# Sinkhorn attention and routed experts on one core: the first w1 load, the order of mixes, batch-0 logits, x sums and PSUM pools rearranged

## The chip, the cores and the metric

The kernel runs on one core of a Trainium2 chip. The metric is device time of one execution in microseconds (us), the median of several runs. A core has five engines that issue independently: TensorE (PE) with its weight loads (PEld), VectorE (DVE), ScalarE (ACT), GpSimd (POOL) and SyncE (SP). The last two also issue the DMAs here, each on a queue of its own. Every engine works through its instructions in the order in which they are queued.

## The reference

Two stages. Attention over 4 batches, 8 heads, 768 positions of 64: a matrix P per head (8 x 8 blocks of 96 positions) is normalised five times by rows and columns, the blocks of k and v are mixed by it, and each block of q attends to its mixed block. Then a mixture of 8 experts over the 3072 resulting rows x of 512, every expert on every row:

```python
k_sorted = np.einsum('bhij,bhjcd->bhicd', P, k_b)
v_sorted = np.einsum('bhij,bhjcd->bhicd', P, v_b)
attn = softmax(scale * q_b @ k_sb.T)          # per block of 96
x = (attn @ v_sb) as [3072, 512]
P = np.exp(x @ w_gate - max)                  # [3072, 8]
for _ in range(8):                            # rows, then columns
    P /= P.sum(1) + 1e-9; P /= P.sum(0) + 1e-9; P *= N / E
for e in range(E):
    out += P[:, e:e+1] * (np.maximum(x @ w1[e], 0) @ w2[e])
```

(Shortened: the softmax stands for the reference's max, exp and division.)

## The kernel before

**Head (0 to 36 us).** Batch 0 of the attention is done at once in two halves b of four blocks each, with pairs of heads hp, on PSUM tiles of two banks each (pool `ps0`, four tiles used in turn, handed out by `pair()`). Its steps are written out by hand in a string (L486): `s` is `half_scores` (matmuls, then the exponential on ACT), `m` is `half_mix` (attention times v, then reciprocal and product on DVE), `t` is `half_turn` (transposes into `xtT`, which holds x transposed), `h` is `half_hidden` (the first layer of expert 0, 256 of its 1024 columns at a time), `v` is `sort_pair` for batch 1 (the mixing of v by P), `k` `wide_keys`, `p` the spreading of P for all batches with the loads of batch 1 and of w2. In `s03` the digits are b and hp; in `h01` b and the group of columns. `unread` names the steps that are preceded by one matmul on a blank tile whose result nobody reads (`warm`).

**The hop.** `sort_values` and `sort_pair` leave the mixed v in `vs` with 16 partitions for each block; `hop` moves it by DMA into `vsbt`, with each block's 96 positions on 96 partitions. For batch 0 it is cut into twelve DMAs, five issued by SP and seven by POOL. POOL's DMA queue has been given before that, in this order: q, v, k of batch 0, `w_gate`, and the first half of w1 of expert 0 (`load_w1(0, 0, 512)`, L99). The rest of w1 and batch 1's v are held behind `gate`, a POOL copy that reads the first two pieces of the hop (L478 to L482).

**Middle (36 to 110 us).** Batches 1 to 3 of the attention, on single banks from a pool of eight (`pa`), are woven with expert 0's layers on the batches before (`first_two`, `weave`, `run_both`). `attention` takes its plan from a string as well (L544, L552): `q` queries, `k` keys, `s` scores, `m` mix, `t` turn, `l` logits; the commas join steps that stand between two steps of the other stream. The logits (x times `w_gate`) of batch 0 are the first work on `pa` (L543).

**Experts 1 to 7.** These use Strassen's form with seven products in place of eight, which needs sums of quarters of x (`sum_x(p)`, p the group of 1024 rows: four DVE instructions, three into `xc`, the fourth in place in `xtT`), of w1 (`sum_w`, POOL), of w2 (`sum_w2`, POOL) and of the hidden layer (`sum_h`, POOL). The first three of `sum_x(0)` are traced in batch 3's part of the loop (L568), the fourth in the first step of the next stage (`works`, L802), which also carries the normalisation of the gate (`balance`, called `chain`) and expert 0 for the last two batches (`last_two`). From there PSUM is split into `bk`, five banks for the first layer, and `op`, three for the second (L583 to L586). The seven experts then follow in one loop, from some 170 us to the end.

**What sets the order.** `pin` is `tc.keep_in_program_order`: the instruction stays behind the one that was traced before it on the same engine. Instructions that are not pinned, `sum_x`'s among them, are put by a scheduler where it takes their engine to be free and their inputs ready, and so may stand far ahead of their place in the text. `reuse_waits="tile"` makes a tile of a new pool wait for those tiles of the old pool that lay on the same memory, and for no others.

Of the kernel before, what the change touches and what calls it, by code (L numbers as in the profile page):

```python
# [17 lines left out]
ALU = mybir.AluOpType  # L18
# [7 lines left out]
def kernel(  # L26
# [11 lines left out]
    nc = tc.nc  # L38
    B, H, S, D = 4, 8, 768, 64
    NB, BL = 8, 96  # L40
    N, Dm, E, F = 3072, 512, 8, 1024
    NT = 24
    TB = S // 128
# [20 lines left out]
    pin = tc.keep_in_program_order  # L64
# [14 lines left out]
    def load_w1(e, f0=0, f1=F):  # L79
        if e not in w1t:  # L80
            w1t[e] = wp.tile([128, 4, F], BF16, name="w1e")
        pin(nc.gpsimd.dma_start(
            out=w1t[e][:, :, f0:f1],
            in_=moe_w1[e].rearrange("(kk k) f -> k kk f", k=128)[:, :, f0:f1]))
# [11 lines left out]
    load_batch(0, [(x, l0, 4) for x in "vk" for l0 in (0, 4)])  # L96
    wg = ones.tile([128, 4, E], BF16)
    pin(nc.gpsimd.dma_start(out=wg, in_=moe_w_gate.rearrange("(kk k) e -> k kk e", k=128)))
    load_w1(0, 0, 512)  # L99
    blank = perp.tile([128, 512], BF16)  # L100
    nc.vector.memset(blank, 0.0)
    mask16 = ones.tile([128, 16], F32)
# [17 lines left out]
    def sum_x(p):  # L120
        if p not in xc:
            xc[p] = xcp.tile([128, 3, 2, 512], BF16, name="xc", bufs=2)
        ta, tb = (slice(1024 * p + 512 * i, 1024 * p + 512 * i + 512) for i in range(2))
        b11, b12, b21, b22 = (xtT[:, k:k + 2, t] for k in (0, 2) for t in (ta, tb))
        x1, x2, x4 = (xc[p][:, j] for j in range(3))
        for a, b, c in ((b12, b11, x1), (b22, x1, x2), (b21, x2, x4), (b22, b12, b12)):
            nc.vector.tensor_tensor(out=c, in0=a, in1=b, op=ALU.subtract)
            yield

    Pb = perp.tile([128, 32, 8], F32)  # L130
# [73 lines left out]
                                  kps.rearrange("p kk (i c) -> p i c kk", i=8))  # L204

    at = {}

    def new_at(bb, hp, h):
        at[bb, hp, h] = sp.tile([128, NB, 96], BF16, name="atp", bufs=8)
# [155 lines left out]
    def attention(bb, bank, plan):  # L365

        def step(what, hp):
            if what == "q":
                queries(bb, hp, bank)
            elif what == "k":  # L370
                keys(bb, hp, bank)
            elif what == "s":
                scores(bb, hp, bank)
            elif what == "t":
                turn(bb, hp, bank, nc.vector.tensor_copy)
            elif what == "l":
                logits(bb, bank, (0, 1, 2) if hp == 0 else (3,))
            else:
                for h in range(2):
                    mix(bb, hp, h, bank)  # L380

        for some in plan.split():
            for x in some.split(","):
                step(x[0], int(x[1]))
            yield
# [41 lines left out]
    with tc.tile_pool(name="ps0", bufs=4, space=bass.MemoryType.PSUM,  # L427
                      reuse_waits="tile") as ps0:
        pair = lambda: ps0.tile([128, 2, 512], F32, name="pair")
        warm(pair(), 11)  # L430
        rs = pp.tile([32, 8], F32)
        cs = pp.tile([32, 8], F32)
        Pt = P.rearrange("p i j -> p j i")
        nc.vector.reduce_max(out=rs, in_=P, axis=AX.X)
        nc.vector.tensor_sub(P, P, mkap(rs, [rs.ap[0], rs.ap[1], [0, 8]]))
        for it in range(5):


            pin(nc.scalar.activation(out=P, in_=P, func=AF.Exp))
            if it == 3:  # L440
                warm(pair(), 3)
            for hp in {2: (0, 1), 3: (2,), 4: (3,)}.get(it, ()):
                wide_queries(hp, pair)
            if it == 1:
                pin(nc.vector.reduce_sum(out=mask16, in_=Ibig.rearrange("p (j c) -> p c j", c=16),
                                         axis=AX.X))
            pin(nc.vector.reduce_sum(out=rs, in_=P, axis=AX.X))
            nc.vector.reciprocal(out=rs, in_=rs)
            nc.vector.tensor_mul(P, P, mkap(rs, [rs.ap[0], rs.ap[1], [0, 8]]))
            nc.vector.reduce_sum(out=cs, in_=Pt, axis=AX.X)  # L450
            if it == 0:
                nc.vector.tensor_scalar_add(cs, cs, 1e-9)
            nc.vector.reciprocal(out=cs, in_=cs)
            nc.vector.tensor_mul(Pt, Pt, mkap(cs, [cs.ap[0], cs.ap[1], [0, 8]]))

        Prep = perp.tile([32, 8, 8, 16], BF16, name="R1")
        for eng, i0, n in ((nc.vector.tensor_copy, 0, 5), (nc.scalar.copy, 5, 3)):
            eng(Prep[:, i0:i0 + n], mkap(P, [P.ap[0], [8, n], [1, 8], [0, 16]], off=i0 * 8))

        def spread(n):  # L460
            t = pair()
            warm(t, n)
            pbps = t[:, 0, 0:256].rearrange("p (i g) -> p i g", i=8)
            for i in range(8):
                pin(nc.tensor.matmul(pbps[:, i, :], Prep[:, i].rearrange("p j c -> p (j c)"),
                                     Ibig[0:32, 0:32], start=True, stop=True))
            return pbps

        build_r(0, nc.vector, 2, spread(12))
        S_, G_ = nc.sync, nc.gpsimd  # L470
        for hp in range(4):
            sort_pair(0, hp, pair)
            if hp == 1:
                hop(0, [(S_, 0, 0, 4), (G_, 1, 0, 4), (S_, 2, 0, 4), (G_, 3, 0, 4)])
        wide_keys(0, pair)
        hop(0, [(S_, 0, 4, 4), (G_, 1, 4, 4), (G_, 2, 4, 4), (G_, 3, 4, 4),
                (S_, 4, 0, 8), (G_, 5, 0, 8), (G_, 6, 0, 8), (G_, 7, 0, 8)])
        gate = nc.gpsimd.tensor_copy(  # L478
            held, mkap(vsbt[0], [[VW, 96], [520, 2]], off=259))
        with tc.issue_after(gate.ins):  # L480
            load_w1(0, 512, F)
            load_batch(1, [("v", 0, 8)])  # L482
        wide_keys(1, pair)
        halves = [mps.tile([128, 8, 384], BF16, name="hTs") for _ in range(2)]
        unread = {"s03": 1, "m00": 1, "m01": 1, "m02": 1, "m03": 1, "m10": 1, "m11": 1}
        for x in ("s00 k2 s01 k3 p s02 s03 s10 m00 s11 m01 s12 m02 s13 m03 t00 m10 m11 t01 m12 "  # L486
                  "h00 m13 h01 t10 h02 t11 h03 v0 v1 v2 v3 h10").split():
            n = [int(c) for c in x[1:]]
            if x[0] == "s":
                half_scores(*n, pair, unread.get(x, 0))  # L490
            elif x[0] == "m":
                half_mix(*n, pair, unread.get(x, 0))
            elif x[0] == "t":
                half_turn(*n, lambda: ps0.tile([128, 2048], BF16, name="pair"),
                          nc.vector.tensor_copy if x == "t11" else nc.scalar.copy)
            elif x[0] == "h":
                half_hidden(*n, halves[n[0]], pair)
            elif x[0] == "v":
                sort_pair(1, *n, pair)
            elif x[0] == "k":  # L500
                wide_keys(*n, pair)
            else:
                nc.vector.tensor_copy(Pb, spread(0).rearrange("p i g -> p g i"))
                build_r(1, nc.gpsimd, 4)
                load_batch(1, [("k", 0, 8), ("q", 0, 4), ("q", 4, 4)])
                load_w2(0)
        hop(1)
# [10 lines left out]
    with ExitStack() as c2:  # L518
        pa = c2.enter_context(tc.tile_pool(name="pa", bufs=8, space=bass.MemoryType.PSUM,
                                           reuse_waits="tile"))  # L520
        bank1 = lambda shape, dt: pa.tile(shape, dt, name="bank", tag="bank")
# [18 lines left out]
                next(a, 0)  # L540
                run(n)

        logits(0, bank1, (0, 1, 2, 3))  # L543
        at1 = attention(1, bank1, "k0 k1 k2 q0 q1 s0 q2 s1 k3 q3 s2 "  # L544
                                  "m0 s3 m1,t0 m2,t1 m3 t2 t3,l0 l3")
        run_both(at1, (1, 1, 1, 1, 0, 1, 0, 1, 0, 0, 2))
# [4 lines left out]
        run_both(at1, (1, 0, 1, 0))  # L551
        usual = "q0,q1,k0 k1,s0,q2 k2,s1,q3 m0 k3,s2 m1,t0 s3 m2,t1 m3 t2 t3,l0 l3"  # L552
        for bb, ns in ((2, (5, 3, 2, 4)), (3, (5, 4, 0, 5))):
            at1 = attention(bb, bank1, usual)
            weave(at1, ex, 5, ns[0])
            if bb + 1 < B:
                load_batch(bb + 1, [(x, 0, 8) for x in "vkq"])
                build_r(bb + 1, nc.gpsimd, 4)
            else:
                load_w1(1)  # L560
                sums = sum_w(1)
            weave(at1, ex, 3, ns[1])
            if bb + 1 < B:
                weave(sort_values(bb + 1, bank1), ex, 5, ns[2])
            else:
                for _ in sums:
                    pass
                x0 = sum_x(0)  # L568
                for _ in range(3):
                    next(x0)  # L570
            weave(at1, ex, 4, ns[3])
        for _ in ex:
            pass
# [6 lines left out]
    osp = late("osp", 1)  # L580
    htp, fsp, hsp, w2q = late("htp", 2), late("fsp", 1), late("hsp", 3), late("w2q", 1)
    h3p = late("h3p", 2)
    bk = ctx.enter_context(tc.tile_pool(name="bk", bufs=5, space=bass.MemoryType.PSUM,  # L583
                                        reuse_waits="tile"))
    op = ctx.enter_context(tc.tile_pool(name="op", bufs=3, space=bass.MemoryType.PSUM,
                                        reuse_waits="tile"))  # L586
    osbl[1] = osp.tile([128, 6, Dm], F32, name="osbl1")
    load_w2(1)
# [294 lines left out]
```

## Time and profile before

| | us |
|---|---|
| median of 3 runs | 675.48 (675.46 to 680.38) |
| the profiled execution, device time | 675.74 |
| its span in the profile | 673.5 |
| PE busy | 660.1 (98%) |
| DVE busy | 544.3 (81%) |
| POOL busy | 473.0 (70%) |
| ACT busy | 296.1 (44%) |

The span runs from the first to the last instruction; device time has 2.2 us more around it. The profile is that of one execution. Its views are: busy time by engine and by stretch; the groups of instructions by source line; the waits, that is, whose idle time was ended by whom; the chain of work that ended last, traced back from the end; the timeline of single instructions; and the DMA issues with the time from issue to landing. `L153` is line 153 of the kernel; `out<-in` names the tiles that an instruction writes and reads. The granted clock of TensorE in this run was 0.999 of full speed over the span.

### The profile page before, as it was taken

To read this page: it belongs to the slowest core of one execution; us is meant where nothing else is said; L and a number is where in the kernel's file an instruction comes from. 1 tells how busy PE (TensorE), PEld (TensorE's weight loads), DVE (VectorE), ACT (ScalarE), POOL (GpSimd) and SP (SyncE) were. 2 spreads that over 40 slices of the span, in tenths; PEclk is the share of its full clock that TensorE was granted. 3 is DMA by queue.
4 is the path that set the end of the run, shared out by engine and by line. 5 is a ranking of instruction groups with operands and counts; after the bars stand their busy time and mean duration, and the time that the engine had idled before them with its cause. 6 is when DMAs were issued, how large, how long until landed. Compare 5 with 4: busy or idle time off the path is not lost.

```text
span 673.5 us, 13293 instructions
## 1 busy us (share of the span) xinstructions
PE 660.1 (98%) x5150; PEld 435.3 (65%) x5150; DVE 544.3 (81%) x1134; ACT 296.1 (44%) x530; POOL 473.0 (70%) x500
## 2 busy tenths in 40 slices
PE   8999999999999999999999999999999999999996
PEld 3656665554666666666666666666666666666675
DVE  6548777663889888888888888988888888888896
ACT  5773863479443434333333334343433334333430
POOL 4713344017897998898897998689886999636745
PEclk9999999999999999999999999999999999999999
DMA  9997964003040340031203040034003220001223
GB/s 158 189 215 133 142 113 64 1 0 54 11 64 6 59 63 1 1 63 29 36 1 63 2 63 1 6 58 63 1 1 65 27 38 1 1 1 62 95 79 142
DMA packets 32800, 36.57 MB, mean 54 GB/s; under 512 B 2097, under 2 KB 25777, under 8 KB 32737
## 3 DMA queue, kind: packets, MB, share of 16 engines
q0 software_dynamic: 26848, 27.57, 26.0%
q1 hardware_dynamic: 5888, 8.15, 3.8%
q8 instruction: 40, 0.66, 0.4%
q14 instruction: 24, 0.19, 0.1%
HBM read 52.45 MB, written 6.29 MB: 87 GB/s over the span
## 4 chain that ended last, share of the span: by engine, by line
PE 73%; DVE 1%; POOL 1%; issue 0%; ACT 0%; DVEq 0%
PE oacc L740 36%; PE bk L653 36%; PE bk L740 1%; DVE osbl L705 1%; POOL hs L723 1%; DVE hT L689 0%; DVE hT L692 0%; ACT p L673 0%; DVEq L705 0%
## 5 line engine op out<-in xcount | busy, mean ns | idle before, releaser
L705 DVE SCALAR_TENSOR_TENSOR osbl<-oacc,glog,osbl 128x256 f32<-128x256 f32 (+1 forms) x490 | 255.2, 521 | 61.6 <-PE oacc L740 61.4
L653 PE MATMUL bk<-xtT,w1e 128*128 128x512 bf16 x504 | 149.7, 379 | 0.0
L723 POOL TENSOR_TENSOR hs<-hT 128x512 bf16<-128x512 bf16 (+2 forms) x105 | 99.4, 959 | 67.6 <-DVE hT L692 67.5
L740 PEld LDWEIGHTS <-hT 128*128 128x128 bf16 x1008 | 98.6, 98 | 64.5 <-issue 1.3
L740 PEld LDWEIGHTS <-hs 128*128 128x128 bf16 x1008 | 98.5, 98 | 64.5 <-POOL hs L723 1.5
L740 PE MATMUL oacc<-w2e,hT 128*128 128x256 bf16 x796 | 119.6, 273 | 0.5 <-ACT hT L695 0.5
L695 ACT ACTIVATE hT<-bk 128x512 bf16<-128x512 f32 x84 | 50.3, 598 | 158.7 <-PE bk L653 158.7
L723 POOL TENSOR_TENSOR hs<-hT,hs 128x512 bf16<-128x512 bf16 (+2 forms) x105 | 99.8, 958 | 4.9
L723 POOL TENSOR_TENSOR hs<-hs,hT 128x512 bf16<-128x512 bf16 (+2 forms) x105 | 99.9, 960 | 4.3 <-ACT hT L695 0.4
L653 PE MATMUL bk<-xc,wc 128*128 128x512 bf16 x336 | 99.9, 379 | 0.2 <-ACT p L673 0.2
L740 PE MATMUL oacc<-w2e,hs 128*128 128x256 bf16 x612 | 92.0, 273 | 0.9 <-POOL hs L723 0.9
L681 ACT COPY u<-bk 128x512 f32<-128x512 f32 x84 | 49.2, 586 | 95.2 <-PE bk L653 94.5
L653 PEld LDWEIGHTS <-w1e 128*128 128x128 bf16 x672 | 65.7, 98 | 10.5
L689 DVE CUSTOM_DVE_ANT_0 hT<-bk,p 128x512 bf16<-128x512 f32 x84 | 58.1, 692 | 11.8 <-ACT p L686 6.4
L699 DVE SCALAR_TENSOR_TENSOR h<-bk,hT 128x512 bf16<-128x512 f32 x84 | 57.1, 680 | 5.8 <-ACT hT L695 5.8
L686 ACT COPY p<-bk 128x512 f32<-128x512 f32 x84 | 49.2, 586 | 23.5 <-PE bk L653 23.5
L673 ACT COPY p<-bk 128x512 f32<-128x512 f32 x84 | 49.3, 587 | 20.1 <-PE bk L653 20.1
L677 DVE CUSTOM_DVE_ANT_0 hT<-bk,p 128x512 bf16<-128x512 f32 x84 | 57.0, 679 | 1.0 <-ACT hT L393 0.6
L692 DVE CUSTOM_DVE_ANT_0 hT<-bk,u 128x512 bf16<-128x512 f32 x84 | 57.1, 679 | 1.0 <-PE bk L653 1.0
L740 PE MATMUL oacc<-w2s,hs 128*128 128x256 bf16 x364 | 54.8, 273 | 0.1
L653 PEld LDWEIGHTS <-wc 128*128 128x128 bf16 x504 | 49.3, 98 | 8.0 <-issue 0.4
L653 PE MATMUL bk<-xtT,wc 128*128 128x512 bf16 x168 | 50.0, 379 | 0.0
(142 smaller groups left out, 838.7 us busy)
## 6 DMA issues: line engine op xcount, KB each, us to landing
w1e<-in_moe_w_dram POOLq DMA_DIRECT2D x7, 1024.0 KB, 8.0
w2e<-in_moe_w_dram POOLq DMA_DIRECT2D x7, 1024.0 KB, 8.8
out_dram<-osbl SPq DMA_DIRECT2D x23, 256.0 KB, 2.0
kvq<-in_v_dram POOLq DMA_DIRECT2D x3, 768.0 KB, 8.5
kvq<-in_k_dram POOLq DMA_DIRECT2D x3, 768.0 KB, 11.1
vsb<-vs SPq DMA_DIRECT2D x17, 97.5 KB, 4.8
kvq<-in_q_dram POOLq DMA_DIRECT2D x4, 384.0 KB, 8.6
kvq<-in_q_dram POOLq DMA_DIRECT2D x2, 768.0 KB, 19.2
```

The source lines that it names most:

```text
L653: hold(nc.tensor.matmul(ps, wa[:, kk, :], xa[:, kk, :], start=(first and kk == 0), stop=(kk == 1), skip_group_check=True))
L673: nc.scalar.copy(p1, u)
L677: nc.vector._custom_dve(TENSOR_ADD_SAT, out=c11, in0=w, in1=p1, s0=TOP, s1=0.0)
L681: nc.scalar.copy(u2, u)
L686: nc.scalar.copy(p5, v)
L689: nc.vector._custom_dve(TENSOR_ADD_SAT, out=c22, in0=u, in1=p5, s0=TOP, s1=0.0)
L692: nc.vector._custom_dve(TENSOR_ADD_SAT, out=c12, in0=v, in1=u2, s0=TOP, s1=0.0)
L695: nc.scalar.activation(out=c21, in_=u, func=AF.Relu)
L699: nc.vector.scalar_tensor_tensor(out=h3[e, p][:, i, :], in0=u, scalar=0.0, in1=c22, op0=ALU.max, op1=ALU.subtract)
L705: nc.vector.scalar_tensor_tensor(out=o, in0=ps, scalar=glog[:, t, e:e + 1], in1=o, op0=ALU.mult, op1=ALU.add)
L723: nc.gpsimd.tensor_tensor(out=c, in0=a, in1=b, op=o)
L740: nc.tensor.matmul(ps, h[:, fb, :], w[:, fb, :], start=(first and fb == 0), stop=(fb == 3), skip_group_check=True)
```

## The change

Five edits:

- The first load of w1 is 256 columns instead of 512; the rest follows behind the gate in two loads (384 and 384) instead of one (512).
- In batch 0 a mix follows each score from the third on (`s02 m00 s03 m01 s10 m02 ...` instead of `s02 s03 s10 m00 s11 m01 ...`), and the unread matmul ahead of `s03` moves to `s13`.
- The logits of batch 0 become a last step `l` of the same string, on a tile of `ps0`, instead of the first work on `pa`.
- `sum_x(0)` is pinned in program order, and its first three instructions become steps `x` of batch 2's plan, behind `q2`, `q3` and `t0`; the fourth stays in the first step of the expert stage.
- `op` is opened before `bk`, so that the two swap places in PSUM.

```diff
-    load_w1(0, 0, 512)
+    load_w1(0, 0, 256)
...
         for a, b, c in ((b12, b11, x1), (b22, x1, x2), (b21, x2, x4), (b22, b12, b12)):
-            nc.vector.tensor_tensor(out=c, in0=a, in1=b, op=ALU.subtract)
+            (pin if p == 0 else lambda ins: ins)(
+                nc.vector.tensor_tensor(out=c, in0=a, in1=b, op=ALU.subtract))
             yield
...
     at = {}
+    x0 = sum_x(0)
...
                 turn(bb, hp, bank, nc.vector.tensor_copy)
+            elif what == "x":
+                next(x0)
...
         with tc.issue_after(gate.ins):
-            load_w1(0, 512, F)
+            load_w1(0, 256, 640)
+            load_w1(0, 640, F)
             load_batch(1, [("v", 0, 8)])
...
-        unread = {"s03": 1, "m00": 1, "m01": 1, "m02": 1, "m03": 1, "m10": 1, "m11": 1}
-        for x in ("s00 k2 s01 k3 p s02 s03 s10 m00 s11 m01 s12 m02 s13 m03 t00 m10 m11 t01 m12 "
-                  "h00 m13 h01 t10 h02 t11 h03 v0 v1 v2 v3 h10").split():
+        unread = {"m00": 1, "m01": 1, "m02": 1, "m03": 1, "s13": 1, "m10": 1, "m11": 1}
+        for x in ("s00 k2 s01 k3 p s02 m00 s03 m01 s10 m02 s11 m03 s12 t00 s13 m10 m11 t01 m12 "
+                  "h00 m13 h01 t10 h02 t11 h03 v0 v1 v2 v3 h10 l").split():
...
+            elif x[0] == "l":
+                logits(0, lambda shape, dt: pair()[:, 0, 0:TB * E].rearrange(
+                    "p (t e) -> p t e", e=E), range(4))
...
-        logits(0, bank1, (0, 1, 2, 3))
...
-            at1 = attention(bb, bank1, usual)
+            at1 = attention(bb, bank1, usual if bb == 3 else usual.replace(
+                "q2", "q2,x0").replace("q3", "q3,x0").replace("t0", "t0,x0"))
...
-                x0 = sum_x(0)
-                for _ in range(3):
-                    next(x0)
...
+    op = ctx.enter_context(tc.tile_pool(name="op", bufs=3, space=bass.MemoryType.PSUM,
+                                        reuse_waits="tile"))
     bk = ctx.enter_context(tc.tile_pool(name="bk", bufs=5, space=bass.MemoryType.PSUM,
-                                        reuse_waits="tile"))
-    op = ctx.enter_context(tc.tile_pool(name="op", bufs=3, space=bass.MemoryType.PSUM,
                                         reuse_waits="tile"))
```

## The prediction

> **What bounds the kernel now.** I read the table of stretches first: where is TensorE (PE) not busy? Columns: the stretch, its length, then busy time and instructions of each engine, granted clock, DMA share, GB/s.
>
> ```profile
> core 0: us, PE busy (x) PEld busy (x) DVE busy (x) ACT busy (x) POOL busy (x), PEclk, DMA share, GB/s
> ...
> 18.00:26.00 8.00, 7.27 (x132) 5.68 (x132) 5.81 (x14) 5.95 (x8) 7.24 (x11) 1.00 0.93 169
> ...
> 110.00:125.00 15.00, 13.94 (x84) 7.75 (x83) 12.12 (x34) 8.66 (x18) 0.00 (x0) 1.00 0.45 69
> 125.00:170.00 45.00, 44.33 (x232) 22.43 (x232) 24.23 (x61) 33.80 (x63) 16.21 (x18) 1.00 0.14 24
> 170.00:660.00 490.00, 489.06 (x3388) 331.04 (x3386) 424.70 (x806) 187.57 (x319) 400.98 (x411) 1.00 0.18 33
> ```
>
> From 170 to 660 us PE is idle for 0.94 us in all (490.00 - 489.06). The chain of waits steps there every 0.868 us, over four matmuls of 256 columns and two of 512: 2048 columns in 0.868 us, 2.36 per ns. No edit takes a matmul out of this loop, so 73% of the span (490 of 673.5) stays. What can move is the head, before 125 us. Next I read PE's own waits up to 130 us (engine, line, waited for: total, times, longest):
>
> ```profile
> PE pair L465 <- DVE R L458: 1.0, 1, 1.0
> PE bank L263 <- ACT hTs L363: 0.9, 1, 0.9
> PE bk L391 <- DVE osbl L408: 0.8, 1, 0.8
> PE pair L333 <- DMA vsb<-vs: 0.6, 2, 0.4
> PE bank L219 <- DVE kTs L203: 0.5, 1, 0.5
> ```
>
> The last four, 0.9 + 0.8 + 0.6 + 0.5 = 2.8 us, are the ones the five edits touch: 0.4% of the time. Then the timeline around each (start, length, engine, line, work; in brackets the idle time before and who ended it). First the hop, then the logits, the sums, the new PSUM pools:
>
> ```profile
> 20.17 0.52 POOL L153 DMA_DIRECT2D vsb<-vs  x1 [0.65 <-DMA w1e<-in_moe_w_dram]
> 20.40 0.33 PE L333 MATMUL pair<-vsb,atp 96*96 96x65 bf16 x4 [0.39 <-DMA vsb<-vs]
> 20.90 0.33 PE L333 MATMUL pair<-vsb,atp 96*96 96x65 bf16 x4 [0.17 <-DMA vsb<-vs]
> ...
> 36.56 0.74 PE L263 MATMUL bank<-wg,xtT 128*128 128x8 bf16 x24 [0.90 <-ACT hTs L363]
> ...
> 66.08 1.23 DVE L127 TENSOR_TENSOR xc<-xtT,xc 128x1024 bf16<-128x1024 bf16 x1
> 67.23 1.98 DVE L203 CAST kTs<-bank 128x384 bf16<-128x384 f32 x4
> 68.33 0.56 PE L219 MATMUL bank<-qTs,kTs 64*96 64x96 bf16 x16 [0.53 <-DVE kTs L203]
> ...
> 110.94 2.11 PE L391 MATMUL bk<-xtT,w1e 128*128 128x384 bf16 x12 [0.79 <-DVE osbl L408]
> ...
> 117.68 0.30 PEld L637 LDWEIGHTS bk<-cs,onesc 128*128 128x128 f32 x2 [0.29 <-DVE cs L634]
> ```
>
> PE issues in order, and from 36 us on it is nearly always full, so what is won ahead stays won unless a transfer or another engine's chain is met earlier.
>
> **Less w1 ahead of the hop, and the new order of mixes.** The 512 KB load of w1, issued at 7.13, lands 12.8 us later (issue to landing of that line alone), at 19.9. The first hop piece, issued on SP at 15.60, takes 4.8 us and lands at 20.4; PE resumes then. The same pieces in batches 2 and 3, at 61.10 and 84.16, take 3.1 and 3.0, and the one issued at 20.17, after w1, takes 2.6. How fast the POOL queue runs: its first two loads (384 KB) are issued at 1.26 and 2.17 and land after 4.9 and 5.9 us, 1.93 us apart, so 256 KB is 1.28 us. With w1 halved the first load ends near 18.5, and a piece issued at 15.60 lands at 15.60 + 3.0 = 18.6 at best, 1.8 earlier. That meets the new order: s02 runs at 18.26, a warm-up matmul at 18.57, and m00 now comes at 18.8 instead of after s03, s10 and another warm-up. PE in 18 to 26 has 8.00 - 7.27 = 0.73 us idle, the most that can go. Warm-up matmuls are seven before and after. I take -0.6; the third row piece (SP, 16.34) may still cost 0.1. If the hop landed as before, two scores and a warm-up (0.31 each from 18.26 to 18.57, 0.23 from 21.46 to 21.69) would move behind the wait: +0.85. Taken nearer the first end, as the 3.0 us rows are of the same pieces.
>
> [...]
>
> What the split moves: POOL issues one more DMA (0.79 us), paid back by the 0.65 us that its last hop piece no longer waits for w1. The bytes behind the gate grow by 256 KB (1.28 us), the gate opens about 0.65 earlier, so every load behind it (v, k, q, w2 on POOL's queue) lands about 0.65 later. The new second piece (384 KB) is wanted by h01, at 27.8 now: the 512 KB at 20.98 landed after 5.4 us, at 26.4, so a smaller one 0.65 earlier is in time. v0 at 32.4 needs v, landed at 30.3 (21.76 + 8.5): 1.5 us of slack against 0.6 + 0.65. Tightest is the second half of w2: issued at 27.84, 19.0 us to landing, 46.8; wanted by the fifth matmul of L400, 47.63 + 0.87 = 48.5. Slack 1.7; taken from it 0.65 by the queue and 1.27 by PE coming earlier (0.6 + 0.67 of the logits). That is -0.2: I charge +0.2, range 0 to +0.9, since the hop of batch 1 also shares the engines then.
>
> **Logits of batch 0.** Today their first bank is that of h10's tile, so PE waits 0.90 for ACT's L363 at 35.70 to 36.51. Put in the tile that v1 freed (DVE casts v1 and v3 from 33.35, 1.82 for the two), 24 matmuls run while ACT reads h10. The keys k0 then take the bank that still waits for ACT, and start at 36.56 instead of 37.23: -0.67. It can't be more (k0 waits for the same ACT), and L267's copy (0.21, DVE, idle 2.17 before) is covered. From 0 to -0.67; I take -0.67.
>
> **x sums in order.** The third sum now sits in DVE's queue at 66.08 and holds the key casts to 67.23; PE's score waits 0.53. In the plan of batch 2 the sums follow q2, q3 and t0, where DVE idled 1.10 (before 70.31), 1.16 (72.52) and 0.60 (78.78) us. Each costs 0.68 to 1.23 (line L127). The first two fit; the third pushes the next reciprocal by up to 0.6, which PE sees only if a bank comes late; 82 us has 1.30 of DVE idle to take it back. -0.5, range -0.6 to +0.1. The fourth moves from 81.04, where nobody waited, to the start of the expert stage. There DVE runs without a break from 110.19 to 115.27 and PE waits 0.29 for its chain at 117.68: +0.2, range 0 to +0.65. Other sums that the scheduler floats there (six from 111.27 to 115.15) may give way, hence not the whole.
>
> **PSUM pools swapped.** bk's first bank is the one that the last keep still reads (110.19 to 110.88), which costs 0.79. Logits of batch 0 leaving this pool already turn its round by one bank, and the swap sets bk on other banks, so the wait should go by either. But the chain after it is DVE's: PE comes 0.79 earlier to L637 and may wait there instead. 0 to -0.79; middle -0.4.
>
> **Sum.** -0.6 + 0.2 - 0.67 - 0.5 + 0.2 - 0.4 = -1.77. The profiled run took 675.74 (span 673.5 and 2.2 around it), 0.26 above the median 675.48. The forecast for the median is 675.48 - 1.77 = 673.7; the span, 671.8.
>
> **Rivals.** (A) The hop lands no earlier, its latency being its own. For: POOL's and SP's pieces take much the same. Against: 2.6 to 3.1 us when nothing is ahead. Then +0.85 stands for -0.6 and w2's slack holds: 0.85 - 0.67 - 0.5 + 0.2 - 0.4 = -0.5, 675.0.
> (B) Slower: as A, and PE, with m00 next in its order, stands still from 18.8 to 20.4. The longest idle time it has had since warming up is 1.0 (before L465), with the clock at 1.00 after it. The first 11 warm-ups took 4.88 us (0.44 each), a later 12 took 2.76 (0.23): a cold stretch of 4.9 us loses 2.4. It decides at the point where 1.6 us idle drops the clock: 675.0 + 2.4 = 677.4. [...]
> (C) The swap does nothing: PE meets DVE's chain. No -0.4, the fourth sum whole, +0.65: -0.6 + 0.2 - 0.67 - 0.5 + 0.65 = -0.92, 674.6. For: the 0.29 already there. Against: floated sums may give way.
>
> **Chances.** Forecast 0.50, C 0.22, A 0.13, B 0.05, and 0.10 for queues ordered anew by the scheduler in ways that no row shows. Every full gain gives 0.73 + 0.67 + 0.6 + 0.79 = 2.8, 672.7; the bad ends (hop 0, w2 +0.9, sums -0.5 and +0.65, pools 0) with -0.67 give +0.4, 675.9. Range 672.4 to 676.3. Within 1% (6.75 us, about what a measurement tells from no change) is every case worked out; only the unseen 0.10 reaches beyond: faster 0.02, slower 0.05, same 0.93.
>
> **What would show it.** L333's first group starting near 18.8 with a wait under 0.5; no w1 wait before POOL's last hop piece; L263 right behind h10 and k0 waiting about 0.3; no wait of L219 on L203 near 68; the first bk matmul without wait, and the wait at the first L637 either about 0.3 (forecast) or near 1 (C). A wait of L400 on w2e over 0.5, or a matmul of 0.44 us after 18 us, would make the number wrong.

## The result, and the profile after

The changed kernel takes 674.48 us (median of 22 runs, 674.07 to 675.05); the kernel before, beside it, 675.66 (22 runs, 675.43 to 680.38). The ratio is 0.9974, with a 95% interval of 0.9963 to 0.9985. Three runs of before stand near 680 us and pull its mean; the medians alone give 674.48 / 675.66 = 0.9983, or 1.18 us less. So the kernel is faster by some 0.2%, well within 1%. The forecast was 673.7, 0.8 too low.

The profiled run of after took 675.05, the slowest of its 22, against 675.74 for the profiled run of before: 0.69 less. The last store is issued at 670.15 in the one and at 670.80 in the other, 0.65 earlier. Where that comes from is read as before: first the table of stretches (stretch, length, busy time and instructions of each engine, granted clock, DMA share, GB/s), here of after.

```profile
core 0: us, PE busy (x) PEld busy (x) DVE busy (x) ACT busy (x) POOL busy (x), PEclk, DMA share, GB/s
...
18.00:26.00 8.00, 7.65 (x136) 6.01 (x134) 6.00 (x15) 6.05 (x9) 8.00 (x12) 1.00 0.98 163
...
110.00:125.00 15.00, 14.03 (x83) 7.64 (x82) 12.60 (x38) 8.66 (x18) 0.00 (x0) 1.00 0.44 68
```

Between 18 and 26 us PE now stands idle for 0.35 (8.00 - 7.65) instead of 0.73. Next PE's own waits in after (engine, line, waited for: total, times, longest). A line of before is one to five numbers lower than the same line of after.

```profile
PE bk L642 <- DVE cs L639: 0.8, 2, 0.5
PE bank L404 <- DMA w2e<-in_moe_w_dram: 0.7, 1, 0.7
...
PE bank L199 <- ACT hTs L365: 0.3, 1, 0.3
PE pair L335 <- DMA vsb<-vs: 0.3, 1, 0.3
```

The 0.9 of the logits, the 0.8 of the first expert matmul and the 0.5 of the score are gone; the hop's 0.6 is 0.3. In their place stand 0.7 for w2 and 0.5 for DVE's `cs` (0.29 before). The timeline of after shows where each falls (start, length, engine, line, work; in brackets the idle time before and who ended it):

```profile
19.23 0.70 PE L335 MATMUL pair<-vsb,atp 96*96 96x65 bf16 x8 [0.30 <-DMA vsb<-vs]
...
35.26 0.74 PE L265 MATMUL pair<-wg,xtT 128*128 128x8 bf16 x24
...
36.32 0.53 PE L199 MATMUL bank<-R,kvq 128*64 128x128 bf16 x12 [0.32 <-ACT hTs L365]
...
46.71 1.02 PE L404 MATMUL bank<-w2e,hTs 128*128 128x512 bf16 x3
48.46 1.02 PE L404 MATMUL bank<-w2e,hTs 128*128 128x512 bf16 x4 [0.72 <-DMA w2e<-in_moe_w_dram]
49.32 0.87 PE L239 MATMUL bank<-vsb,atp 96*96 96x65 bf16 x16
...
67.70 0.56 PE L221 MATMUL bank<-qTs,kTs 64*96 64x96 bf16 x16
...
109.36 2.41 PE L395 MATMUL bk<-xtT,w1e 128*128 128x384 bf16 x12
109.56 0.69 DVE L412 COPY osbl<-bank 128x512 f32<-128x512 f32 x1 [0.68 <-PE bank L404]
...
116.49 0.50 DVE L639 TENSOR_REDUCE cs<-glog 128x8 f32<-128x192 f32 x1
117.04 0.39 PE L642 MATMUL bk<-cs,onesc 128*128 128x8 f32 x2 [0.51 <-DVE cs L639]
```

Held against the same steps of before, this is a ledger of PE's lead. At batch 1's first keys (L199 at 36.32, 37.24 before) it is 0.92. At the first mix of batch 1 (L239 at 49.32, 49.35 before) it is 0.03: the wait for the second half of w2 took it all. The scores (67.70 for 68.33) bring 0.63, and the first expert matmul (109.36 for 110.94) shows 1.58. At L642 it is 0.64 again (117.04 for 117.68): the chain of DVE that makes `cs` took 0.94 of the 0.95 won at L395. From there to the end nothing changes: the first second-layer gather of DVE after 169 us starts at 169.52 for 170.16, the last at 669.64 for 670.29, 0.64 and 0.65.

### The profile page after: what moved, and what is told of

Same layout as the page of the kernel before. It is cut to its first block, busy times and chain, and to the rows that moved or that the text cites. A ratio compares the mean times of both kernels' runs of the same rounds, so it can differ in the third digit from the quotient of the medians.

```text
span 673.2 us, 13219 instructions
## 1 busy us (share of the span) xinstructions
PE 656.5 (98%) x5074; PEld 435.4 (65%) x5150; DVE 544.2 (81%) x1134; ACT 295.9 (44%) x530; POOL 473.1 (70%) x501
## 4 chain that ended last, share of the span: by engine, by line
PE 72%; DVE 1%; issue 1%; POOL 1%; ACT 0%; DVEq 0%
PE oacc L745 37%; PE bk L658 34%; PE bk L745 1%; DVE osbl L710 1%; POOL hs L728 1%; DVE hT L694 0%; DVE hT L697 0%; ACT p L678 0%; DVEq L710 0%
## 5 line engine op out<-in xcount | busy, mean ns | idle before, releaser
L658 PE MATMUL bk<-xtT,w1e 128*128 128x512 bf16 x475 | 143.5, 379 | 0.9
L658 PE MATMUL bk<-xc,wc 128*128 128x512 bf16 x319 | 96.3, 379 | 0.6 <-ACT p L678 0.2
L658 PE MATMUL bk<-xtT,wc 128*128 128x512 bf16 x159 | 48.0, 379 | 0.0
```

What stands on the lines that cost most here:

```text
L658: hold(nc.tensor.matmul(ps, wa[:, kk, :], xa[:, kk, :], start=(first and kk == 0), stop=(kk == 1), skip_group_check=True))
```

## The experiments

Each ran beside the kernel before on the same chip; diffs are against the changed kernel unless said otherwise. The table gives the start of six steps of PE in each profiled run (us), and the median of the runs (12 each; 22 for after) less the median of before on that chip (35 runs, 22 for after). "m00" is the first mix of batch 0, "k0" batch 1's first keys, "mix" its first mix, "score" the score that waited for the key casts, "bk" the first expert matmul, "cs" the first matmul on `cs`.

| kernel | m00 | k0 | mix | score | bk | cs | median, against before |
|---|---|---|---|---|---|---|---|
| before | 20.40 | 37.24 | 49.35 | 68.33 | 110.94 | 117.68 | 0 |
| after | 19.23 | 36.32 | 49.32 | 67.70 | 109.36 | 117.04 | -1.18 |
| r_after (the same again) | 19.02 | 36.08 | 48.87 | 67.26 | 108.92 | 116.59 | -1.14 |
| e13, split alone | 19.79 | 36.46 | 48.68 | 67.66 | 110.27 | 117.01 | -0.46 |
| e9, swap alone | 20.31 | 37.21 | 49.32 | 68.31 | 109.97 | 117.60 | -0.17 |
| e2, no swap | 19.20 | 36.75 | 48.86 | 67.25 | 108.91 | 116.58 | -0.89 |
| e3, logits back | 19.15 | 36.88 | 49.18 | 67.56 | 109.22 | 116.90 | -0.69 |
| e7, x sums back | 19.02 | 36.09 | 49.14 | 68.13 | 110.74 | 117.48 | -0.52 |
| e5, old mixes | 19.82 | 35.78 | 48.24 | 66.62 | 108.29 | 115.96 | -1.12 |
| e6, all sums pinned | 19.06 | 36.14 | 48.55 | 66.93 | 108.58 | 115.71 | -1.34 |
| f1, e5 and e6 | 19.75 | 35.73 | 48.40 | 66.79 | 108.45 | 115.58 | -1.51 |
| e12, half of w1, filled | 20.39 | 37.61 | 49.72 | 68.11 | 109.77 | 117.44 | -0.02 |
| e1, half of w1 | 20.46 | 41.93 | 54.04 | 72.43 | 114.09 | 121.76 | +4.47 |

e4 has no full row, as it splits that mix; its median is -0.98. How far single profiles differ can be read from kernels that are alike: after, r_after, e2, e4, e6 and e7 have the same head, and their k0 lies between 36.08 (r_after) and 36.75 (e2). So a difference under some 0.7 at one place of one profile shows nothing by itself. The way from one step to the next is steadier where no transfer is waited for: after, r_after and e2, whose engines work through the same instructions, take 18.38 to 18.39 from mix to score and 7.67 to 7.68 from bk to cs. Their medians lie at -1.18, -1.14 and -0.89, so differences under 0.3 in the last column show nothing either.

**e1: half of w1 ahead of the hop again**, everything else of the change kept.

```diff
-    load_w1(0, 0, 256)
+    load_w1(0, 0, 512)
...
-            load_w1(0, 256, 640)
-            load_w1(0, 640, F)
+            load_w1(0, 512, F)
```

> The changed kernel with the first load of w1 at 512 columns again and one load of 512 behind the gate; the new order of mixes and all else stay. Theory 1 (the bytes of w1 ahead of the hop set when the hop lands): m00 waits until about 20.4 us as in the kernel before, a wait of some 1.5 us in place of 0.30, and w2's second half lands near 46.8 again, so that the wait for w2 at L404 (0.72 in the profile of the changed kernel) goes. Net: PE at 49 us is 0.85 - 0.67 = 0.2 us later than before the change, the whole kernel 0.2 to 0.6 us slower than the changed one (674.7 to 675.1). Theory 2 (the hop's latency is its own): m00 still starts at 19.2 and the kernel is 0.4 to 0.7 us faster than the changed one, having lost the wait for w2 alone.

Measured: 680.17 (678.15 to 681.86), ratio 1.0057 with an interval of 1.0039 to 1.0075. Neither theory had that. Timeline of e1 at the hop, then its stretches:

```profile
18.61 0.39 PE L326 MATMUL pair<-blank 128*128 128x512 bf16 x1
20.46 0.68 PE L335 MATMUL pair<-vsb,atp 96*96 96x65 bf16 x8 [1.46 <-DMA vsb<-vs]
```

```profile
20.00:22.00 2.00, 1.51 (x25) 1.25 (x24) 0.79 (x2) 0.51 (x1) 1.65 (x4) 1.00 0.73 174
22.00:24.00 2.00, 2.00 (x28) 1.52 (x26) 1.32 (x5) 1.10 (x2) 1.99 (x3) 0.57 0.85 81
24.00:26.00 2.00, 2.00 (x25) 1.61 (x23) 1.25 (x3) 1.03 (x2) 2.00 (x3) 0.50 1.24 204
...
30.00:32.00 2.00, 2.00 (x16) 1.31 (x15) 1.44 (x3) 0.80 (x1) 0.43 (x1) 0.50 1.32 204
32.00:36.50 4.50, 4.50 (x45) 3.02 (x44) 0.89 (x2) 2.44 (x4) 0.00 (x0) 0.94 1.31 203
```

PE waits 1.46 us for the hop, and then the granted clock (the number ahead of the DMA share) is 0.50 while PE is busy all the time. From the means, it falls at about 22.3 (0.57 over 22 to 24) and is back at about 32.5 (0.94 over 32 to 36.5): 10.2 us at half speed. All twelve runs show it: their granted clock over the whole execution is 0.988 to 0.993, where before mostly has 0.998 to 1.000. That is rival B's mechanism.

**e12: e1, with the wait filled.** Eight unread matmuls ahead of m00 instead of one.

```diff
-        unread = {"m00": 1, "m01": 1, "m02": 1, "m03": 1, "s13": 1, "m10": 1, "m11": 1}
+        unread = {"m00": 8, "m01": 1, "m02": 1, "m03": 1, "s13": 1, "m10": 1, "m11": 1}
```

> The kernel with 512 columns of w1 ahead of the hop and the new order of mixes (680.17 us), with eight instead of one unread matmul ahead of m00, seven more of some 0.22 us each, so that TensorE works through the 1.46 us in which it waited for the hop. Theory 1 (the 5 us come from the clock, which falls to half when TensorE stands still in that wait: 0.50 granted from about 23 to 33 us): with the wait filled the clock stays at 1.00, the hop still lands at 20.4, and the time is 675 to 675.5. Theory 2 (the 5 us come from something that the late hop delays, and the clock follows): still near 680.

Measured: 675.47 (675.22 to 675.81), ratio 0.9989 (0.9973 to 1.0005). Each against before on its own chip, that is 4.5 less than e1 (-0.02 and +4.47). Timeline and stretch of e12:

```profile
18.54 1.90 PE L326 MATMUL pair<-blank 128*128 128x512 bf16 x8
20.39 0.33 PE L335 MATMUL pair<-vsb,atp 96*96 96x65 bf16 x4
```

```profile
22.00:24.00 2.00, 2.00 (x39) 1.62 (x36) 1.82 (x5) 1.66 (x3) 1.99 (x3) 1.00 0.68 84
```

m00 starts no earlier than in e1, but the clock stays at 1.00 and PE gets 39 matmuls done where e1 got 28. So the idle time, not the late data, made the 4.5. The late data alone cost 674.35 to 675.47, 1.1 (r_after ran on the same chip).

**e13: the split of w1 alone**, on the kernel before (the diff of e1 read from below to above).

> The kernel before with the split of w1 (256, then 384 and 384 behind the gate) as its only edit. Theory 1 (the split alone is worth 0.7 us, since the old order meets the hop without a wait): m00 starts near 19.9 without a wait in place of 20.40, the second half of w2 lands near 47.5 and is met at 47.8, just in time, and the kernel is 0.5 to 0.8 us faster than the kernel before. Theory 2 (w2, 0.65 later, takes it back): within 0.2 us of the kernel before. If the kernel before falls to a lower clock in its executions near 680, for want of work in the same wait, none of these 12 is near 680.

Measured: 675.31 (674.95 to 675.93), ratio 0.9992 (0.9984 to 1.0). Timeline of e13, first mix:

```profile
19.79 0.51 PE L333 MATMUL pair<-vsb,atp 96*96 96x65 bf16 x8
```

With the old order two scores stand ahead, so m00 comes later than in after, yet it waits for nothing, and k0 is 0.78 earlier than before (36.46 for 37.24). The lead at `cs` is 0.67 (117.01); in the median it is 0.46.

**e5: the old order of mixes**, the split and all else kept.

```diff
-        for x in ("s00 k2 s01 k3 p s02 m00 s03 m01 s10 m02 s11 m03 s12 t00 s13 m10 m11 t01 m12 "
+        for x in ("s00 k2 s01 k3 p s02 s03 s10 m00 s11 m01 s12 m02 s13 m03 t00 m10 m11 t01 m12 "
```

(and the unread matmul at `s03` again, not at `s13`).

> The changed kernel with the old order in batch 0 (s03 and s10 ahead of m00) and the old places of the unread matmuls; the quarter of w1 stays. Theory 1 (what counts is that the hop lands by 19.5; with that the old order has work to the moment it lands): m00 starts near 19.9 without a wait and the time is within 0.2 us of the changed kernel. Theory 2 (the new order is what wins): PE is 0.3 us or more later at the keys k0 than in the changed kernel (36.6 in place of 36.3), and the kernel 0.2 us or more slower.

Measured: 674.37 (673.93 to 676.42), ratio 0.9978 (0.996 to 0.9996), against 674.35 of r_after on the same chip. k0 comes at 35.78, 0.30 earlier than in r_after, and at 35.73 in f1, which has the old order too: both lie ahead of all six kernels that share after's head. So the new order wins nothing and may cost some 0.3 at k0; what the hop gains is the split's.

**e3: the logits back on the pool `pa`.**

```diff
-                  "h00 m13 h01 t10 h02 t11 h03 v0 v1 v2 v3 h10 l").split():
+                  "h00 m13 h01 t10 h02 t11 h03 v0 v1 v2 v3 h10").split():
...
+        logits(0, bank1, (0, 1, 2, 3))
```

> The changed kernel with the logits of batch 0 as the first work on the bank pool again, all else as changed, the swap too. Theory 1 (w2's second half is what the head runs into): PE is 0.67 us later at the keys k0 (37.0 in place of 36.3), the wait for w2 at L404 shrinks from 0.72 by the same, and from 49 us on nothing is different: 674.4 to 674.7. Theory 2 (the logits' gain stands by itself): 0.67 us slower, 675.1. In both the first matmul of bk has no wait on the last keep, as bk no longer begins on that bank.

Measured: 675.01 (674.74 to 675.58), ratio 0.9982 (0.9966 to 0.9998). Timeline of e3:

```profile
36.20 0.74 PE L265 MATMUL bank<-wg,xtT 128*128 128x8 bf16 x24 [0.90 <-ACT hTs L365]
```

The 0.90 for ACT is back, as before, and k0 starts at 36.88, 0.56 later than in after. But the wait for w2 is down from 0.72 to some 0.2 (the matmuls of L404 at 47.27 take 2.07 us, those of L400 in before, without a wait, 1.89), and the mix is 0.14 earlier than in after. Of what the logits win at k0, 0.2 (against e2, which has them moved, on the same chip) to 0.5 (against after) reaches the median; the 0.2 is not clear of the noise.

**e4: the second half of w2's first output tile behind the first mix of batch 1.**

```diff
-        run_both(at1, (1, 1, 1, 1, 0, 1, 0, 1, 0, 0, 2))
+        run_both(at1, (1, 1, 1, 1, 0, 1, 0, 1, 0, 0, 1))
...
-        run_both(at1, (1, 1, 1, 2))
+        run_both(at1, (2, 1, 1, 2))
```

> The changed kernel with one step of the middle moved: the second half of the first output tile of expert 0 (the four matmuls that wait for the second half of w2) comes behind the first mix of batch 1 instead of ahead of it. Theory 1 (the 0.72 us wait at L404 for w2 takes back what the hop and the logits won): the wait falls below 0.1, the mix may wait up to 0.3 for the last piece of batch 1's hop, which lands near 47.6, and the kernel is 0.4 to 0.7 us faster than the changed one: 673.8 to 674.1. Theory 2 (what is won there is lost again further on, at q's load of batch 2 or at DVE's chain at 117 us): the time stays within 0.1 of 674.5.

Measured: 674.72 (674.32 to 678.92), ratio 0.9981 (0.9959 to 1.0003): no gain (-0.98 against before; e2, on the same chip, -0.89). PE's waits in e4:

```profile
PE bank L239 <- DMA vsb<-vs: 0.4, 1, 0.4
```

The wait for w2 is gone, and the mix waits for batch 1's own hop in its place. Two transfers land together near 48 us: PE goes on with the mix at 48.48 here, when the hop's last piece is there, and with w2's second half at 48.46 in after.

**e2: `bk` opened ahead of `op` again**, all else of the change kept. Each engine runs the same instructions in the same order as after.

```diff
+    bk = ctx.enter_context(tc.tile_pool(name="bk", bufs=5, space=bass.MemoryType.PSUM,
+                                        reuse_waits="tile"))
     op = ctx.enter_context(tc.tile_pool(name="op", bufs=3, space=bass.MemoryType.PSUM,
                                         reuse_waits="tile"))
-    bk = ctx.enter_context(tc.tile_pool(name="bk", bufs=5, space=bass.MemoryType.PSUM,
-                                        reuse_waits="tile"))
```

> The changed kernel with bk opened before op again, all else as changed. Every engine's queue is the same as in the changed kernel. Theory 1 (the batch-0 logits having left the bank pool already turn its round by one, so the swap is not needed): the first matmul of bk starts without a wait, as in the changed kernel, and the time is the same within 0.1 us (674.4 to 674.6). Theory 2 (the swap does it): a wait of 0.8 us on L412 is back at 110 us. Even then the time may stay, because PE next waits for DVE's chain at L642 (0.51 in the changed kernel): that wait would shrink by as much.

Measured: 674.81 (674.14 to 675.02), ratio 0.9978 (0.9962 to 0.9994). From the mix on its row in the table is that of r_after to 0.01, bk without a wait included. In this company the swap does nothing.

**e9: the swap alone**, on the kernel before (the diff of e2 read the other way).

> The kernel before with op opened ahead of bk as its only edit. Theory 1 (DVE's chain takes the swap's gain): the first matmul of bk has no wait in place of 0.79, the wait at the first L637 grows from 0.29 to about 1.0, and the time stays within 0.15 of the kernel before. Theory 2 (half of it stays): 0.4 us faster than the kernel before; all of it: 0.8.

Measured: 675.60 (675.36 to 680.31), ratio 0.999 (0.997 to 1.001). Timeline of e9:

```profile
109.97 2.11 PE L391 MATMUL bk<-xtT,w1e 128*128 128x384 bf16 x12
...
117.60 0.39 PE L637 MATMUL bk<-cs,onesc 128*128 128x8 f32 x2 [0.47 <-DVE cs L634]
```

Here the swap does take away the wait of 0.79 (109.97 for 110.94), and 7.6 us later 0.08 is left of it, after 0.28 more at L620 and 0.47 at L637. It is worth nothing measurable.

**e7: the x sums for the first rows as before**, neither pinned nor moved (the diff of the change, those lines undone).

> The changed kernel with the sums of x for the first rows unpinned and traced in batch 3's part again, as before the change. Theory 1 (the third sum ahead of the key casts costs 0.5 to 0.6 us): the wait of L221 on the casts is back near 67 us at 0.5, and the kernel is 0.4 to 0.6 us slower than the changed one: 674.8 to 675.0. Theory 2 (the fourth sum, which then leaves the start of the expert stage, gives it back in DVE's chain): within 0.2 us of the changed kernel.

Measured: 675.25 (674.77 to 679.7), ratio 0.9989 (0.9972 to 1.0006). Timeline of e7:

```profile
68.13 0.56 PE L219 MATMUL bank<-qTs,kTs 64*96 64x96 bf16 x16 [0.53 <-DVE kTs L203]
...
110.74 2.11 PE L393 MATMUL bk<-xtT,w1e 128*128 128x384 bf16 x12 [0.78 <-DVE osbl L410]
```

The score's 0.53 is back, as both theories had it, and the median, each against its own before, is 0.66 above after and 0.37 above e2. What nobody expected is the second line: with the pools swapped and the logits gone from `pa`, the first expert matmul waits for the last keep again.

**e6: all sums of x pinned**, those for the other rows too.

```diff
-            (pin if p == 0 else lambda ins: ins)(
+            pin(
```

> The changed kernel with the sums of x for the other two groups of rows pinned too, so that none of the six stands in DVE's queue ahead of the first steps of the gate's normalisation (five did, 0.69 us each, from 111.3 to 115.2). Theory 1 (the swap's 0.79 us was taken back by DVE's chain, which these sums lengthen): the wait of 0.51 at the first L642 falls below 0.1 and the kernel is 0.4 to 0.6 us faster than the changed one. Theory 2 (pinned sums now stand between later steps of the chain or of the experts and are waited for there): no faster, or up to 0.7 us slower.

Measured: 674.15 (674.05 to 674.83), ratio 0.9972 (0.9956 to 0.9988), 0.20 under r_after on the same chip, which is not clear of the noise. Timeline of e6:

```profile
115.71 0.36 PE L642 MATMUL bk<-cs,onesc 128*128 128x8 f32 x2
```

Without the floated sums in DVE's way, PE finds `cs` ready. From bk to cs it takes 7.13 (115.71 - 108.58) instead of the 7.67 of r_after. The lead over before then shrinks, from 1.97 at cs to 1.67 at 170 us and 1.57 at the last gather. f1, the other kernel with all sums pinned, loses as much (2.10, 1.79, 1.68), and r_after keeps its own (1.09, 1.09, 1.10). So of the 0.54 that the pins win between bk and cs, some 0.4 is lost again later, as theory 2 had it; the views above don't show where.

**f1: e5 and e6 together.**

> The changed kernel with the old order of mixes and with all sums of x pinned, the two edits that each left PE earlier than the changed kernel did in their profiles (by 0.30 at the keys k0, by 0.52 at the first L642). Theory 1 (both gains are on PE's path): the wait at the first L642 is gone, k0 starts near 35.8, and the time is 673.5 to 673.9. Theory 2 (w2 and batch 1's hop, which land near 47.4 whatever PE does before, take back the first; something in the expert loop takes back a part of the second, as the median of the pinned kernel, 674.15 against 674.35, suggests): 674.1 to 674.3.

Measured: 674.26 (673.86 to 674.72), ratio 0.9972 (0.9959 to 0.9985). Against its own before it is the lowest of all (-1.51; e6 -1.34, r_after -1.14), but its interval and theirs overlap: not shown to be better.

**r_after: the changed kernel again**, on the chip of e12, e6 and e5, as their yardstick.

> The changed kernel itself, as the reference for the three that run with it. In its first runs the median was 674.48 us and none of 22 executions was near 680; the same is expected here, 674.4 to 674.8, as the kernel without the swap, whose queues are the same, took 674.81.

Measured: 674.35 (674.06 to 675.06), ratio 0.9974 (0.9958 to 0.999); the first result again.

## Why the prediction was right, and which of its steps were not

**Logits, -0.67: right, then spent.** L265 follows h10 without a wait, and k0 waits 0.32 for ACT where about 0.3 was forecast. k0 leads by 0.92 in after; with 0.67 of it for the logits, 0.25 is left for the hop.

**Hop, -0.6: right for the split, not for the order.** The split alone brings 0.78 at k0 (e13). In after m00 starts at 19.23 with a wait of 0.30, between the 18.8 I gave as best and the 20.40 of before; the new order seems to give about 0.3 back (e5 against r_after: 35.78, 36.08), and what is left for the hop is 0.25 in after and 0.49 in r_after. The mechanism was off in two places, in opposite directions. I had w1 end near 18.5, from 1.28 us for its 256 KB; it ended at 17.4, 2.5 earlier than before. And I had the piece stand behind all of w1 and land 3.0 after its issue at best. It took 3.6 (issued at 15.56) with w1 ending at 17.4, and 4.8 before with w1 ending at 19.9: 1.8 and 4.3 us of w1 still to come. So the piece, measured by those 3.0, is late by a third to two fifths of what is left of w1 (0.6 of 1.8, 1.8 of 4.3). It does not stand behind all of w1: in before, from 17.4 to 18.6 us, with w1 still to land at 19.9, POOL's queue moved 185 packets and SP's 132. (SP issues four of the twelve pieces and POOL eight, not five and seven as the description of the hop has it.)

**w2, +0.2: the size that failed.** I counted a slack of 1.7 against 1.92 taken from it. In after the second half of w2 was waited for 0.72, in r_after 0.52, in e3 some 0.2, in e2 not at all; over 0.5 is the sign I had named of a wrong number. PE came for it 0.92 earlier (L404 begins at 46.71, L400 at 47.63), less than the 1.27 I had counted; what I had much too small is how far the landing moves. It landed at 46.8 in before and at 48.5 in after, 1.6 later and not 0.65. That is the split's doing: in e13, which has no other edit, PE goes on with w2's second half at 47.8, held up for 0.1 (the matmuls of L400 at 46.85 take 1.99 us, in before 1.89). Wherever a kernel with the split shows that PE was held up there, it goes on between 47.4 (e5) and 48.5 (after). So the same edit that brings the hop forward puts w2 back.

The table shows what that does: where PE waits for nothing, the mix follows k0 by 12.1 us (before, e2, e12: 12.11), and every kernel whose k0 is before 36.4 takes longer: 13.00 in after, 12.79 in r_after, 13.05 in e7, 12.46 in e5. The mix doesn't start before 48.2 in any row, however early k0 is. Taking w2 out of the way left the hop in it (e4). So transfers set a floor near 48 us, which itself moves by a microsecond from kernel to kernel (48.24 in e5, 49.32 in after). What sets it beside the split (all loads of batch 1, w2 and the hop share the engines from 26 us on at a DMA share above 1: 1.26 in before and 1.27 in after from 26 to 48.5) is read from the table of stretches and was not tested by itself. In after, all but 0.03 of what the hop and the logits won ends there; in r_after, 0.48 of 1.16 is left.

**x sums, -0.5: right.** The score's wait is gone, and the step from mix to score is 18.38 (67.70 - 49.32) instead of 18.98: -0.60. e7 puts it back and costs 0.4 to 0.7 in the median.

**Fourth sum, +0.2, and swap, -0.4: the step that failed.** "0 to -0.79; middle -0.4" stood between PE meeting DVE's chain and not. It met it: the wait at bk went, 0.95 of lead with it, and from bk to cs PE took 7.68 instead of 6.74, 0.94 more. That is rival C's mechanism, and the swap alone (e9) shows it without the other edits: 0.97 earlier at bk, 0.08 at cs. DVE's rows tell why. In before they begin and end so:

```profile
110.19 0.69 DVE L408 COPY osbl<-bank 128x512 f32<-128x512 f32 x1 [0.68 <-PE bank L400]
...
117.12 0.51 DVE L634 TENSOR_REDUCE cs<-glog 128x8 f32<-128x192 f32 x1
```

DVE comes to `cs` by a queue that is nearly full from the last keep on: from the one to the other it takes 6.93 in before and 6.93 in after (109.56 to 116.49), of which it is busy for 6.27 and 6.79, whether bk waits (0.79 in before) or not. In e9 PE starts the four matmuls ahead of the last keep at 109.11 for 109.13, bk 0.97 earlier, and `cs` 0.08. So an earlier bk brings `cs` no further forward; an earlier last keep does, and its lead in after (0.63) is the lead at cs (0.64). That DVE's floated sums are what fills the queue is shown by e6: once they are pinned PE has no wait at `cs` (115.71), and bk to cs takes 7.13 instead of 7.67. The fourth sum cost nothing that shows: r_after and e9, with it and without it there, take 7.67 and 7.63; on DVE's 6.93 us there is a wait of 0.52 for ACT in before (L630 at 115.79), and none in after.

My reason that the wait "should go by either" of logits and swap, since the logits turn the round of the pool by one bank, falls with e7: both edits are in, and the wait of 0.78 is there. In e2 it is gone without the swap. Which bank the last keep holds depends on all that the scheduler placed earlier; that is inferred from where the wait comes and goes, not read from the banks.

**The sum.** -0.67 and -0.25 at k0, +0.89 at the mix, -0.60 at the score, -0.95 at bk, +0.94 at cs: -0.64, against 0.69 in the time of the profiled run. The median run does better, 1.18, and r_after's profile with a lead of 1.09 at cs is nearer to it. Of the forecast's six terms the logits and the x sums came as forecast; by the ledger of after, hop, w2 and swap were some 0.35, 0.7 and 0.4 worse, and the fourth sum 0.2 better. That the median lies between 672.4 and 676.3 says little for the sum, as that range also holds the time of before.

**Rivals.** A did not happen: the hop came 1.2 earlier. (The pieces that take much the same are, in before, SP's first with 4.8 us and POOL's with 4.2.) C gave 674.6 by the right mechanism at the swap, though not for its fourth sum, and 674.48 was measured: the nearest of the numbers, in part by luck, as it had w2 at 0.2 and charged 0.65 for a sum that cost nothing. B did not happen in the change, and no wait in the head of before shows the drop of the clock that it supposes (1.00 in all stretches up to 36.5 us); e1 shows one, to 0.50 after 1.46 us of idle time. B's bounds were too kind: I forecast that the slow stretch would last 4.9 us and cost 2.4; in e1 it lasted 10.2 and cost 4.5. With the new order and without the split, the change would have been slower than before.

## What to carry to other kernels

Ask of every gain ahead of a transfer what lands next: here nearly all of 0.9 us won by 36 us ended in a wait for a transfer near 48, which one of the winning edits had itself put back, and 0.95 won at 110 ended in another engine's queue 8 us later; neither wait stood in the list of before at that size. Edits that look separate can hold each other up: the new order of mixes was worth nothing, but harmless only with the split: without it the kernel was 4.5 us slower than before. So run the parts alone and each part undone, and where TensorE has to wait for a transfer in the head, try work that nobody reads: in a wait of 1.46 us it was worth 4.5 us here.

## What the runs showed of the hardware that was not expected

An idle time of 1.46 us between bursts (e1) was followed by a granted clock of 0.50 from about 22.3 to 32.5, in a kernel whose PE was busy throughout those 10.2 us; an idle time of 0.96 before L465, up to 12.65 us in before, was not: the granted clock there is 1.00 from 12.65 to 18. Where between the two it turns, and whether the length alone decides, no run shows. Filling the 1.46 us with seven more matmuls of about 0.22 us kept the clock at 1.00 (e12).

Single executions of other kernels have a lower granted clock, too. Where that of every execution is on record, it is 0.988 to 0.993 in e1's twelve; it is 0.991 to 0.995 in 11 of 105 of before and in one of 12 of e9, 0.992 or 0.993 in 3 of the 130 of the ten kernels with the split (two of e4, one of e7), and 0.998 or more in all others. So it is rarer with the split. Whether it strikes at the hop in these too, when that comes late, stays open, as none of them was profiled.
